# Token mixing and SwiGLU on one core: the taps of the next pair all put among the products, two splits of the first pair put behind three sums, and a new joined order of products and output steps

## The chip, the cores and the metric

The kernel runs on one core of a Trainium2 chip. The metric is the device time of one execution in microseconds (us). The execution shown in the profile took 2447.03 us; three unprofiled runs took 2442.12, 2444.20 and 2449.53 us (median 2444.2).

## What is computed

```python
# lightweight convolution: x is (8, 4096, 192), weight is (8 heads, 7 taps)
w = softmax(weight, axis=-1)
out[b, s, head] = sum over k of w[head, k] * x_pad[b, s + k, head]   # causal, 6 zeros ahead
# then, over the 32768 tokens x of 192 numbers:
xn  = x / sqrt(mean(x * x) + 1e-6) * rms_g
g   = xn @ w_gate            # 192 -> 1536
val = xn @ w_val
return (silu(g) * val) @ w_out   # 1536 -> 192
```

All of it is float32 in and out.

## The kernel before

**Tiling.** The tokens are cut into 32 pairs of 2 x 512 tokens. For a pair, the 1536 hidden columns are six groups j = 0 to 5, each with two blocks of 128 columns. A pair needs 68 products into the hidden columns (six matmuls each, L948) and then 42 output steps (twelve matmul instructions each, L976). Groups 0, 2, 4 and 5 use seven-product forms of Strassen's kind (items P and Q), groups 1 and 3 use the plain form (items A, B, E). The inputs of the products are split into three float32r terms so that sums of the three are exact enough: a high part, a remainder and a second term.

**Joined list.** `LINE` (L131) gives the order of TensorE's 68 products and 42 steps in a pair; a word such as `P7.0` is product P7 of group 0, and `o3.4` is output step form 3 of group 4. TensorE works through this list pair after pair.

**Written order.** `FIRST` (pair 1), `SECOND` (pair 2) and `ORDER` (every later pair) are lists of words that `run` (L1301) emits one after the other. `p3` emits the next three items of the joined list. Every other word goes into the queue of one engine (V VectorE, A ScalarE, G GpSimd, S the sync queue that issues DMAs). A queue is worked in the order in which the words stand, and each instruction waits only for its data and buffers. A trailing `+` means that the word belongs to the next pair, `++` to the one after, `-` to the previous one. So while pair w is multiplied, VectorE also prepares pair w+1, and finishes pair w-1.

The words that matter here:

- `cv0` to `cv6`: the seven taps of the convolution (L470 on ScalarE for `cv0`, L474 on VectorE). Each reads the loaded tokens `xh` and adds into `y`; all wait for the loads `ld.0` to `ld.7` (L174, one per head). Behind the last tap follow `sq`, `red`, `pow`, `bc`, `mul` (the normalisation, in place in `xh`), then `pl.0` to `pl.7` (L1098, eight DMAs that put the heads into DRAM) and `ft.0`, `ft.2`, `ft.4`, `ft.5` (L676, the fetch of the transposed tokens `xb`).
- `x1` to `x4`: sums of token blocks into `tt` (L868). Operands 0, 1 and 2 of the products are token blocks, operands 3 and 4 are these sums.
- `n.i`, `l.i`, `d.i`: the three terms of operand i (ScalarE cast L705, VectorE L854, VectorE L856). A product multiplies with the high part first, then with `l`, then with `d`.
- `f1`, `f3`, `f4`, `f5`, `f6`: copies and sums between banks of products (L705, L1025, L1018); `ga` to `gd` (L1031) and `ma` to `md` (L1038): silu and multiplication of a finished bank, which gives the bank back.
- `h1` to `h4` (L1003): sums of hidden blocks, which the output steps read.
- `c1`, `s7`, `c2` (copies) and `C22`, `C21` (L1055): sums of output banks; `C21` gives back the bank `Z`. `T11`, `T12`, `T21`, `T22` (L991): transposition of finished outputs into `o_sb`; `T12` gives back the bank `X`.
- `st.g.i` (written `Sst0.1-`, L1087): the stores of the previous pair's `o_sb`. In the last pair the stores go out as soon as both transpositions of a half have run (`at_end`, L1069), three on ScalarE's queue and two on the sync queue.
- Split weights sit in DRAM and are loaded into a ring of 12 slots, one piece ahead of its use (`ring_load`, L814): 48 loads in a pair, each behind the last use of its slot.

Two `o_sb` buffers rotate, one for each half of the pair, so a transposition waits for the stores that read the buffer last.

Of the kernel before, what the change touches and what calls it, by code (L numbers as in the profile page):

```python
# [20 lines left out]
def kernel(  # L21
# [58 lines left out]
    )  # L80
    ORDER = (
# [15 lines left out]
    )  # L97
    SECOND = (
# [15 lines left out]
    )  # L114
    FIRST = (
# [14 lines left out]
    )  # L130
    LINE = (  # L131
# [7 lines left out]
    )  # L139

    cst = ctx.enter_context(tc.tile_pool(name="cst", bufs=1))
# [1213 lines left out]
```

## Time and profile before

| | |
|---|---|
| profiled execution, own time | 2447.03 us |
| its span | 2445.2 us |
| around the span | 1.8 us |
| three runs | 2442.12, 2444.20, 2449.53 us |
| TensorE granted clock, whole span | 0.999 |
| busy: TensorE, VectorE, ScalarE, GpSimd | 2427.2, 2089.3, 1034.0, 565.7 us |

A row of a timeline reads: start in us, length in us, engine, line, operation, output and inputs; in brackets how long the engine stood idle before it and who ended the wait. Rows of one kind that follow each other are merged (x2, x3). A row of the chain of waits reads: start, length, what the end of the execution hung on in that time. Names of tiles are shared: `part` is also the space of the three terms of an operand, `ring` also that of pair 2's tokens. Times of successive VectorE rows overlap by some hundredths, so the distance from one start to the next is what an instruction costs the queue.

### The profile page before, as it was taken

The numbers are of one execution on the slowest core, as the hardware profiler recorded it, in microseconds if no ns is written. First come the engines' busy times: TensorE is split into PE (matmuls) and PEld (weight loads), VectorE is DVE, ScalarE is ACT, GpSimd is POOL, SyncE is SP. The second block draws the span as 40 slices with busy tenths as digits, with TensorE's granted clock in tenths as the row PEclk, the third lists the DMA queues.
The fourth block names the chain that finished last, engine by engine and source line by source line (L and its number), as shares of the span: only waits on it lengthen the run. The fifth ranks groups of instructions, "written<-read, shape, count | busy, mean of one in ns | idle before, by whom it ended". The sixth has DMA issues, their size and how long they took to land.

```text
span 2445.2 us, 69382 instructions
## 1 busy us (share of the span) xinstructions
PE 2427.2 (99%) x29136; PEld 1978.5 (81%) x29136; DVE 2089.3 (85%) x2702; ACT 1034.0 (42%) x1431; POOL 565.7 (23%) x482
## 2 busy tenths in 40 slices
PE   8999999999999999999999999999999999999998
PEld 5647888888888888888788898888888788888886
DVE  9678888889888899888898888898888898888974
ACT  6443344444344444344444444443444443444432
POOL 0542122211222211222211222211222112222111
PEclk9999999999999999999999999999999999999999
DMA  7375678777788677778677787777786777876753
GB/s 153 61 212 145 168 177 215 191 170 176 171 186 216 184 170 173 173 196 206 177 173 171 173 210 194 173 175 171 179 215 181 169 173 172 197 204 179 175 155 83
DMA packets 716392, 430.55 MB, mean 176 GB/s; under 512 B 510330, under 2 KB 702386, under 8 KB 716082
## 3 DMA queue, kind: packets, MB, share of 16 engines
q1 hardware_dynamic: 712336, 425.21, 70.7%
q8 instruction: 230, 3.77, 0.7%
q10 hardware_dynamic: 3746, 0.92, 0.2%
q14 instruction: 80, 0.66, 0.1%
HBM read 366.96 MB, written 58.98 MB: 174 GB/s over the span
## 4 chain that ended last, share of the span: by engine, by line
PE 97%; DVE 1%; DMA 1%; SPq 1%; issue 0%; ACT 0%; DVEq 0%; ACTq 0%
PE ps L948 57%; PE ps L976 35%; PE ps L920 2%; PE ps L1135 2%; SPq L174 1%; DMA ht<-in_moe_w_val_dram 0%; DVE part L854 0%; DMA x<-in_x_dram 0%; DVE ht L1003 0%; DMA xh<-in_x_dram 0%; DMA ht<-in_moe_w_gate_dram 0%; SPq L258 0%; DVE part L856 0%; DVE y L474 0%; DVE ht L1038 0%
## 5 line engine op out<-in xcount | busy, mean ns | idle before, releaser
L948 PE MATMUL ps<-part,ring 64*128 64x512 f32 x11160 | 1305.3, 387 | 0.1
L948 PEld LDWEIGHTS ps<-part,ring 64*128 64x128 f32 x11160 | 1108.5, 184 | 161.7 <-issue 5.6
L1031 ACT ACTIVATE tt<-ps 128x512 f32<-128x512 f32 x744 | 441.8, 598 | 683.8 <-PE ps L948 614.8
L1038 DVE TENSOR_TENSOR ht<-ps,tt 128x512 f32<-128x512 f32 x744 | 497.7, 685 | 208.8 <-ACT tt L1031 200.2
L976 PE MATMUL ps<-ht,wo_sb 128*32 128x384 f32 (+2 forms) x7272 | 430.3, 380 | 0.0
L976 PE MATMUL ps<-ht,x 128*32 128x256 f32 (+2 forms) x6696 | 413.1, 379 | 2.8 <-DVE ht L1003 2.6
L976 PEld LDWEIGHTS ps<-ht,wo_sb 128*32 128x32 f32 x7272 | 321.5, 110 | 94.7 <-issue 12.6
L976 PEld LDWEIGHTS ps<-ht,x 128*32 128x32 f32 x6696 | 298.4, 110 | 86.5 <-DVE ht L1003 3.2
L474 DVE SCALAR_TENSOR_TENSOR y<-xh,tp,y 128x1536 f32<-128x1536 f32 x186 | 337.2, 1813 | 3.9 <-ACT y L470 3.5
L503 POOL TENSOR_SCALAR r<-r 128x8 f32<-128x8 f32 x31 | 6.2, 198 | 1431.7 <-DVE r L498 1431.6
L1025 DVE TENSOR_TENSOR ps<-ps,tt 128x1024 f32<-128x1024 f32 x210 | 258.3, 1230 | 36.9 <-ACT tt L705 24.8
L705 ACT COPY ps<-ps 128x1024 f32<-128x1024 f32 (+1 forms) x151 | 134.0, 887 | 274.6 <-PE ps L948 130.1
L1003 POOL TENSOR_TENSOR hs<-ht 128x512 f32<-128x512 f32 x120 | 155.8, 1298 | 169.3 <-DVE ht L1038 127.9
L705 ACT COPY tt<-ps 128x384 f32<-128x384 f32 (+1 forms) x182 | 151.9, 835 | 89.6 <-PE ps L976 79.6
L705 ACT CAST part<-tt 128x1024 fp32r<-128x1024 f32 x60 | 62.8, 1047 | 287.4 <-DVE tt L868 287.4
L1003 DVE TENSOR_TENSOR ht<-ht 128x512 f32<-128x512 f32 x252 | 168.6, 698 | 6.8 <-PE ps L976 6.6
L1003 POOL TENSOR_TENSOR ht<-ht 128x512 f32<-128x512 f32 x120 | 154.4, 1299 | 2.3
L976 PE MATMUL ps<-hs,x 128*32 128x256 f32 (+2 forms) x2232 | 145.2, 379 | 0.0
L948 PE MATMUL ps<-part,part 64*128 64x512 f32 x912 | 128.8, 386 | 0.0
L976 PEld LDWEIGHTS ps<-hs,x 128*32 128x32 f32 x2232 | 106.3, 110 | 24.1
L856 DVE SCALAR_TENSOR_TENSOR part<-part,xb 128x1024 fp32r<-128x1024 f32 x87 | 105.6, 1214 | 0.0
L854 DVE TENSOR_TENSOR part<-xb,part 128x1024 fp32r<-128x1024 f32 x87 | 103.3, 1214 | 0.0
(137 smaller groups left out, 1619.4 us busy)
## 6 DMA issues: line engine op xcount, KB each, us to landing
ring<-wd SPq DMA_DIRECT2D x1326, 192.0 KB
xb<-xd SPq DMA_DIRECT2D x60, 512.0 KB
xd<-xh SPq DMA_DIRECT2D x240, 96.0 KB
part<-wd SPq DMA_DIRECT2D x114, 192.0 KB
xh<-in_x_dram SPq DMA_DIRECT2D x192, 105.0 KB
xb<-xd SPq DMA_DIRECT2D x60, 256.0 KB
out_dram<-o_sb SPq DMA_DIRECT2D x126, 96.0 KB
out_dram<-o_sb SPq DMA_DIRECT2D x62, 128.0 KB
```

Source lines behind the costliest of these rows:

```text
L474: nc.vector.scalar_tensor_tensor(out=y, in0=xk, scalar=w, in1=y, op0=ALU.mult, op1=ALU.add)
L705: nc.scalar.copy(out=dst, in_=src)
L854: e.tensor_tensor(out=split_of(g, 1).bitcast(F32R), in0=src, in1=high, op=ALU.subtract)
L856: nc.vector.scalar_tensor_tensor(out=split_of(g, 2).bitcast(F32R), in0=high, scalar=1.0 + SPLIT, in1=src, op0=ALU.mult, op1=ALU.subtract,)
L920: nc.tensor.matmul(out=self.both(j, c)[:, h, :], lhsT=wf[HALF[h], k, 2 * HOME[j] + f, :], rhs=rb[HALF[h], k, g, :], start=(k == 0), stop=( ...
L948: nc.tensor.matmul(out=self.both(j, c)[:, h, :], lhsT=left[HALF[h]], rhs=right[HALF[h]], start=(first and q == 0), stop=True, skip_group_c ...
L976: nc.tensor.matmul(out=self.acc(b)[i * Q : (i + 1) * Q, at : at + n], lhsT=left, rhs=cols, start=fresh, stop=True, skip_group_check=True, ...
L1003: engine[eng].tensor_tensor(out=dst, in0=a, in1=b, op=op)
L1025: nc.vector.tensor_tensor(out=self.both(j, c), in0=self.both(j, "b"), in1=s5, op=ALU.add)
L1031: nc.scalar.activation(out=tt[:, t, :], in_=self.both(j, c)[:, 0, :], func=AF.Silu)
L1038: nc.vector.tensor_tensor(out=self.hv(j, "abcd".index(c)), in0=self.both(j, c)[:, 1, :], in1=tt[:, t, :], op=ALU.mult,)
L1135: nc.tensor.matmul(out=bank(h, bks[h])[:], lhsT=wf[HALF[h], AT[h][k], u * NF + f, :], rhs=xb[HALF[h], g, k, :], start=(k == 0), stop=(k == ...
```

## The change

`ORDER` is written anew. Two kinds of words change their place by more than a few items. The tap `cv4`, which stood at the end of the list behind `C22` for the pair after next (`Vcv4++`), now stands among the next pair's products (`Vcv4+`); five of the six VectorE taps have another place. The split `l.4` stands at the end of the list and `d.4` at the head of the next, where it was the other way round. `C21` no longer has a tap ahead of it. The transpositions come in the order T22, T21, T12 (before: T12, T21, T22). The token sum `x3` moves ahead of the last multiplications; fetches stand earlier, and the store `st1.2` of the previous pair at the very end, behind all loads of `x`. `SECOND` follows the same pattern. In `FIRST`, `Vd.1+` and `Vl.2+` move behind `Vh1.5`, `Vh3.5` and `Vh2.5`. `LINE` keeps the same items in another order. The number of instructions of each kind does not change.

```diff
     ORDER = (
-        "p3- p1 Vcv5+ Af1.0 p1 VT12- p1 VT21- p1 Vcv1+ VT22- Aga.1 p1 Vma.1 Vl.4 p1 Aga.0 p1",
-        "Af3.0 Vma.0 p4 Vf4.0 p1 Agb.1 Sst0.1- p3 Vcv2+ Vmb.1 p2 Vf5.0 Sst0.2- Agc.0 p1 Vmc.0",
-        "Agd.1 p2 Vmd.1 Agd.0 p2 Agb.0 p1 Vcv6+ Vmb.0 Sst0.3- Vmd.0 p1 Vcv3+ Af1.2 p1 Sst1.0-",
-        "p1 Agc.1 Vmc.1 p1 Sst0.4- Af3.2 Vf4.2 p3 Sst0.0- p1 Aga.2 Sst1.1- p1 Vma.2 Vf5.2 p1",
-        "Asq+ Agc.2 p1 Vred+ p1 Vmc.2 Agd.2 p2 Agb.2 p1 Vmd.2 Gpow+ Agb.3 p1 Vmb.2 p1 Af1.4",
-        "Vmb.3 Vbc+ p2 Gmul+ Aga.3 p1 Spl.4+ p1 Af3.4 Vma.3 p2 Vf4.4 Spl.2+ p1 Spl.7+ Aga.4",
-        "p1 Vma.4 Vh1.1 Spl.5+ p2 Vf5.4 Spl.1+ p1 Agd.3 Vmd.3 Sst1.3- p2 Gh1.0 Agc.4 Spl.3+",
-        "Vmc.4 p1 Spl.0+ Agd.4 p1 Af1.5 Sst1.4- Gh1.3 Agb.4 Gh3.0 Spl.6+ Vmd.4 p1 Gh3.1 Vmb.4",
-        "p2 Sft.0+ Af3.5 Sft.2+ p1 Sft.4+ Gh1.2 p2 Vf4.5 Sld.4++ p2 Sft.5+ Aga.5 Vma.5",
-        "Sld.3++ p1 Agc.3 p1 Vf5.5 Gh3.3 Gh1.4 Vh3.2 p1 Sld.7++ Vmc.3 p2 Vf6.5 Agc.5 p2 Agb.5",
-        "Agd.5 Sld.6++ p1 Vmb.5 p1 Vmd.5 Vmc.5 p1 Vh1.5 Sld.5++ p1 Gh3.4 Vh2.0 Sst1.2- p3 Ac1",
-        "p1 Vh2.3 An.0+ Vh3.5 p2 Vh2.2 Gh2.1 p1 Vx3+ Sld.0++ Vh2.4 p2 Vd.0+ An.1+ p1 Vl.1+",
-        "Vl.0+ p1 Sld.2++ Vx1+ Vh2.5 Vx2+ p2 An.3+ As7 Vh4.2 Vh4.0 Vh4.3 p2 VT11 p1 An.2+ p1",
-        "Vh4.4 Sld.1++ p1 Vh4.1 Vd.2+ p1 Vh4.5 Vl.2+ Vl.3+ Ac2 p2 Vd.1+ p3 Vx4+ p2 An.4+ p1",
-        "Vd.3+ Acv0++ p1 VC22 Vd.4+ Vcv4++ p5 VC21",
+        "Vcv5+ VT22- p1 Af1.0 p2 Vcv3+ p1 VT21- p1 VT12- p1 Vcv1+ Aga.1 p1 Vma.1 Af3.0 Vd.4",
+        "Vf4.0 p3 Vcv4+ p1 Aga.0 p1 Vma.0 p5 Agb.1 Sst0.3- Vmb.1 Sst0.1- Agc.0 Vf5.0 Vmc.0 p2",
+        "Agd.1 Vcv2+ p2 Agb.0 Sst1.3- Sst0.2- Agd.0 Vmd.1 Vmb.0 Vh1.1 p1 Vmd.0 p1 Af1.2 p1",
+        "Vcv6+ p1 Agc.1 Vmc.1 p4 Af3.2 Vf4.2 Aga.2 p1 Vma.2 Vf5.2 p1 Sst1.1- Asq+ p3 Vred+ p2",
+        "Agd.2 Agc.2 Vmd.2 Gpow+ p1 Agb.2 Vmc.2 p2 Vmb.2 Agb.3 p1 Af1.4 Sst0.4- Vmb.3 p1 Vbc+",
+        "p1 Aga.3 p1 Gmul+ p1 Spl.0+ Af3.4 p1 Spl.4+ Spl.3+ Vma.3 Aga.4 p1 Vf4.4 p1 Gh1.2",
+        "Sst1.4- Vma.4 p2 Spl.2+ Spl.1+ Vh3.2 p1 Agd.3 Spl.5+ p1 Agc.4 Spl.6+ Vf5.4 Vmd.3 p1",
+        "Spl.7+ Vmc.4 p2 Agd.4 Sft.0+ Sft.2+ p1 Gh1.3 Sld.5++ Af1.5 Vmd.4 p2 Agb.4 Af3.5 p1",
+        "Sld.7++ Vmb.4 Sft.4+ Sst0.0- p1 Sft.5+ p1 Sld.4++ Vf4.5 p1 Aga.5 Gh3.1 p1 Agc.3 p2",
+        "Vma.5 p1 Gh1.0 Sst1.0- Vf5.5 p1 Sld.3++ Vmc.3 Vf6.5 p2 Vx3+ Gh1.4 p2 Agb.5 Agd.5",
+        "Vmb.5 Agc.5 p2 Vmd.5 p1 Gh3.3 Gh3.0 Vmc.5 Vh1.5 p3 Sld.1++ An.0+ p1 Ac1 Vh3.5 Vx1+",
+        "p1 Vh2.3 Vd.0+ p1 Gh3.4 p3 Vh2.2 Vh2.0 An.1+ p1 Vx2+ Gh2.1 An.3+ Vh2.5 p2 Sld.6++ p1",
+        "Vd.1+ p1 Vh4.5 p2 As7 Sld.0++ An.2+ Vh2.4 Vh4.0 Sld.2++ p1 Vl.1+ p1 Vh4.2 Vl.0+",
+        "Vh4.3 VT11 p2 Vh4.4 Vd.2+ p1 Vl.3+ Ac2 Vh4.1 p2 Vl.2+ p3 Vx4+ p1 Vd.3+ p3 An.4+ VC22",
+        "p1 Acv0++ p3 Vl.4+ p2 VC21 p1 Sst1.2-",
     )
     SECOND = (
...
     FIRST = (
...
-        "An.2+ p1 Vd.3+ p1 Agb.5 Vd.2+ Vmb.5 Sld.0++ p1 Vl.3+ p2 Vl.1+ Agc.5 Vmc.5 Vd.1+ p1",
-        "Sld.1++ Vl.2+ p6 Sld.2++ Agd.5 p1 Vmd.5 Gh2.0 Gh2.4 Gh2.2 Gh2.3 Gh2.1 p1 Vh1.5 p2",
-        "Ac1 Sld.3++ Vh3.5 Vh2.5 Sld.4++ Sld.5++ Sld.6++ Sld.7++ Acv0++ An.0+ An.4+ Gl.0+",
+        "An.2+ p1 Vd.3+ p1 Agb.5 Vd.2+ Vmb.5 Sld.0++ p1 Vl.3+ p2 Vl.1+ Agc.5 Vmc.5 p1 Sld.1++",
+        "p6 Sld.2++ Agd.5 p1 Vmd.5 Gh2.0 Gh2.4 Gh2.2 Gh2.3 Gh2.1 p1 Vh1.5 p2 Ac1 Sld.3++",
+        "Vh3.5 Vh2.5 Vd.1+ Vl.2+ Sld.4++ Sld.5++ Sld.6++ Sld.7++ Acv0++ An.0+ An.4+ Gl.0+",
         "Vd.0+ p4 Vh4.5 p1 Vh4.0 R p3 As7 p6 Ac2 Vh4.3 Vcv1++ Vcv2++ p8 Vh4.2 p2 Vh4.1 p2",
         "VC21 p1 Vh4.4",
     )
     LINE = (
-        "P1.0 Aa.1 Ea.1 Ba.1 P2.0 Q1.0 P5.0 P6.0 Ab.1 Eb.1 Bb.1 Ad.1 P3.0 P7.0 Q2.0 Ed.1 Bd.1",
+        "P1.0 Aa.1 Ea.1 Ba.1 P2.0 P5.0 P6.0 Q1.0 Ab.1 Bb.1 Eb.1 P7.0 Q2.0 P3.0 Ad.1 Bd.1 Ed.1",
...
-        "o2.4 o7.0 o6.2 o6.4 o6.1 o6.5 o4.1 o6.0 o4.0 o4.4 o5.4 o5.5 o5.0 o5.2 o4.5 o5.1 o5.3",
-        "o4.3 o4.2 o3.4 o3.3 o3.1 o3.0 o3.2 o3.5",
+        "o6.1 o6.0 o6.5 o2.3 o6.3 o2.1 o6.4 o4.2 o4.4 o5.1 o5.4 o5.0 o5.3 o4.3 o5.5 o5.2 o4.5",
+        "o4.1 o4.0 o3.2 o3.4 o3.1 o3.0 o3.5 o3.3",
     )
```

38 rows, old and new, of tables (LINE, SECOND) are left out of this document.

## Prediction

> **What bounds the kernel now.** I read the page's first part, then the chain of waits in order of time, TensorE's waits, and then timelines where the chain leaves TensorE.
>
> ```profile
> span 2445.2 us, 69382 instructions
> PE 2427.2 (99%) x29136; PEld 1978.5 (81%) x29136; DVE 2089.3 (85%) x2702; ACT 1034.0 (42%) x1431; POOL 565.7 (23%) x482
> ```
>
> TensorE is busy 99% of the span and the change removes none of its instructions, so only its 18 us of idle time, delays that count as busy, and the ends of the run can change. The chain shows pair after pair as 46.5 us of products and 27.4 us of output steps:
>
> ```profile
> 288.36 46.50 PE ps L948 x408
> ...
> 953.90 46.51 PE ps L948 x408
> ...
> 1101.99 46.50 PE ps L948 x408
> ...
> 1167.45 4.32 DMA xh<-in_x_dram
> ...
> 1175.50 0.48 DVE tt L1055
> ...
> 1176.02 47.15 PE ps L948 x408
> ...
> 1918.84 47.15 PE ps L948 x408
> ...
> 2363.68 46.53 PE ps L948 x408
> ```
>
> An undisturbed pair takes (953.90 - 288.36) / 9 = 73.95 us. The 28 pairs from 288.36 to 2363.68 take 2075.32 us, and 28 x 73.95 = 2070.6: scattered delays cost only 4.7 us in this execution. Two product stages, at 1176.02 and 1918.84, are 0.64 us longer each: 1.3 us. The first shows its cause: the token load lands at 1167.45 + 4.32 = 1171.77, 69.8 us after that pair began; tap 0 on ScalarE follows, then a tap on VectorE, and only behind it `C21` (L1055), which gives the next products their bank. I cannot put the other 3.4 us down to one cause.
>
> **First pair: `d.1` and `l.2` go behind three sums.** TensorE's waits and both timelines around 190 us:
>
> ```profile
> PE ps L976 <- DVE ht L1003: 2.6, 2, 1.4
> 184.48 9.71 POOL L1003 TENSOR_TENSOR ht<-hs,ht 128x512 f32<-128x512 f32 x5 [7.53 <-PE ps L976]
> 187.43 1.71 DVE L856 SCALAR_TENSOR_TENSOR part<-part,ring 128x1024 fp32r<-128x1024 f32 x1
> 192.00 1.07 DVE L1003 TENSOR_TENSOR hs<-ht 128x512 f32<-128x512 f32 x1
> 193.10 1.64 DVE L1003 TENSOR_TENSOR ht<-ht 128x512 f32<-128x512 f32 x1
> 194.80 1.51 PE L976 MATMUL ps<-ht,x 128*32 128x384 f32 x24 [1.35 <-DVE ht L1003]
> 194.85 2.67 DVE L1003 TENSOR_TENSOR ht<-hs,ht 128x512 f32<-128x512 f32 x1
> 197.57 4.76 PE L976 MATMUL ps<-ht,x 128*32 128x384 f32 x84 [1.26 <-DVE ht L1003]
> L1003 DVE TENSOR_TENSOR ht<-ht 128x512 f32<-128x512 f32 x252 | 168.6, 698 | 6.8 <-PE ps L976 6.6
> ```
>
> TensorE wants `h3.5` at 194.80 - 1.35 = 193.45, and `h2.5` two steps (2 x 27.4 / 42 = 1.3) later, at 194.76. Afterwards `md.5` starts at 187.43, where `d.1` did, the sums start at about 188.05 (L1038 takes 0.64, below), and with the durations above (1.07, 1.64, 2.67) `h3.5` is ready at about 190.8 and `h2.5` at 193.5. Both waits go: -2.6 us. The two splits then run until about 197.5, the time at which the sums ended before (194.85 + 2.67), since the queue holds the same work; TensorE needs them in pair 2's second group of products, after 213. The bound: if each sum takes the dearest duration (2.67), `h2.5` is ready at 188.05 + 3 x 2.67 = 196.06, 1.3 us late, and 1.3 are won. I take 2.6, since the sums run beside the same GpSimd work (busy until 194.2) as in the rows.
>
> [...]
>
> **The end of the run.** With the order T22, T21, T12 the half that is complete early is stored early.
>
> ```profile
> 2437.70 0.65 DVE L991 STREAM_TRANSPOSE o_sb<-ps 128x256 f32<-128x256 f32 x2 [3.34 <-PE ps L976]
> 2438.18 4.29 ACTq L1087 DMA_DIRECT2D out_dram<-o_sb  x6
> ```
>
> Before, VectorE stood 3.34 us idle, from 2434.4, because `T12`, which waits for TensorE's last step, stood first; then ten stores went out together, six on ScalarE's queue (4.29 us, 0.72 each), and 2445.2 - 2442.47 = 2.7 us later the span ended. Afterwards T22 and T21 run in the idle time (at most 0.65 us each), three of the six are issued from about 2435.5 to 2437.7, and three remain behind `T12`: 3 x 0.72 = -2.1 us. The bounds are 0 (should the landing of the last store set the end) and -2.7 (should the stores also land sooner).
>
> **The steady part.** The stages of an undisturbed pair and its queues (in steps of 73.95 from 288.36 it began at 510.2, the next at 584.15):
>
> ```profile
> 556.70:584.10 27.40, 27.40 (x507) 20.91 (x506) 26.89 (x36) 8.87 (x11) 1.30 (x1) 1.00 0.73 140
> 555.68 1.22 DVE L1018 TENSOR_TENSOR ps<-ps,tt 128x1024 f32<-128x1024 f32 x1
> 579.54 1.21 DVE L856 SCALAR_TENSOR_TENSOR part<-part,tt 128x1024 fp32r<-128x1024 f32 x1
> 580.68 1.80 DVE L474 SCALAR_TENSOR_TENSOR y<-xh,tp,y 128x1536 f32<-128x1536 f32 x1
> 582.41 0.54 DVE L1055 TENSOR_TENSOR tt<-ps,tt 128x384 f32<-128x384 f32 x1
> 584.60 0.63 DVE L991 STREAM_TRANSPOSE o_sb<-ps 128x256 f32<-128x256 f32 x2
> 587.93 0.64 DVE L1038 TENSOR_TENSOR ht<-ps,tt 128x512 f32<-128x512 f32 x1
> 590.24 1.22 DVE L1025 TENSOR_TENSOR ps<-ps,tt 128x1024 f32<-128x1024 f32 x1
> 579.01 1.58 ACT L470 ACTIVATE y<-xh,tp 128x1536 f32<-128x1536 f32 x1
> 541.01 0.58 SPq L1098 DMA_DIRECT2D xd<-xh  x1
> 552.37 3.45 SPq L676 DMA_DIRECT2D xb<-xd  x2
> 561.19 2.00 ACT L705 CAST part<-xb 128x1024 fp32r<-128x1024 f32 x2
> ```
>
> In the output stage VectorE is busy 26.89 of 27.4 us; a tap there costs 582.41 - 580.68 = 1.73. Taking `cv4` out lets `C21` end 1.73 us sooner than at 582.95, at 581.2; its last input comes a few steps earlier in the new list, so it may be 0.3 sooner still, 580.9. `d.4` against `l.4` is an exchange of 1.2 for 1.2. In an undisturbed pair `C21` was in time anyway, so this wins nothing.
>
> What the tap costs among the products: VectorE's queue from `C21` on is now cv5, T22, cv3, T21, T12, cv1, `ma.1`, `d.4`, `f4.0`, cv4, `ma.0`. From 580.9: four taps 4 x 1.73, three transpositions 3 x 0.63, `ma.1` 0.64, `d.4` 1.14 (580.68 - 579.54), `f4.0` 1.22, `ma.0` 0.64, in all 12.45, ending at 593.35. The product that needs the bank of `ma.0`, `Ad.1`, is the 15th of the new list: 584.15 + 14 x 46.51 / 68 = 593.7. The margin is 0.35 us, somewhat more since rows that follow each other overlap. `f4.0` ends at 592.7 less the tap `cv4`, 591.0, and `P7.0`, the 12th, comes at 591.7. So nothing waits, but these margins are thin. Behind `ma.0` the list repeats the old distances.
>
> The token sum `x3` now stands behind `f6.5` (555.68 + 1.2 = 556.9) and ahead of the last multiplications, where it stood 5 us later. It needs fetch 0. Before, 19 DMAs from 541.01 to the fetch at 552.37 took 0.60 each; the new list has 14 there (eight puts, five ring loads, a store), so the fetch goes out at about 549.4. The cast that reads it ran at 561.19, at most 8.8 us after its issue, which bounds the landing at 558.2, 1.3 us late; the other bound is 0.5 MB at the 140 GB/s of this stage, 3.7 us, or 553.1. I take the latter, since the cast stood behind another copy and not behind the DMA.
>
> The store `st1.2` goes behind the loads of `x`, where only T22 of the next window waits for it, and two 96 KB stores move into the stretch of the loads from ahead of it; one ring load (192 KB) leaves that stretch. So the tokens land no later, and tap 0 may end some 0.65 us later than at 580.59 (0.3 until `cv5`, and the 0.35 above). Before, tokens that landed at 69.8 us, 1.0 after the usual start of tap 0 (579.01 - 510.2 = 68.8), cost 0.64. I take 1.0 of the 1.3 us of late loads as won, bounds 0 and 1.3, and leave the other 3.4 as they are, bounds 0 and -3.4.
>
> **The sum.** -2.6 - 2.1 - 1.0 = -5.7 on the execution's own 2447.0 (2445.2 and 1.8 around it): 2441.3. Without its 4.7 us of scatter that execution would be at 2442.3, and the fastest run took 2442.12; the median run, 2444.2, therefore holds about 2 us of scatter, of which the same share, 1.0 / 4.7, is 0.4. Against the median: 2444.2 - 2.6 - 2.1 - 0.4 = **2439.1**.
>
> **Rivals.** (1) *VectorE too late among the products (slower).* Its place is the 0.35 us before `Ad.1`. If tap 0 ends more than 0.65 us later than now in ordinary pairs, or `x3` holds up the queue as by the bound, every further microsecond recurs in 29 pairs, since VectorE has no idle time from `x3` to `ma.0`. At `x3`'s bound, 1.3 - 0.35 = 0.95 us: 2439 + 28 = 2467. For it speaks how dense the queue is; against it that the fetch goes out 3 us sooner.
> (2) *Only the end is won.* The sums take their dearest durations (1.3 of 2.6) and late loads stay as they are: 2444.2 - 1.3 - 1.2 = 2441.7, and 2444 if the landing of the last store sets the end. The steady order, for all its moves, is then worth nothing, as the gapless chain suggests. [...]
> (3) *The scatter goes as well.* If earlier fetches and the later store thin out the DMA traffic so that no delay is left, the median comes down to the floor: 2442.2 - 4.7 = 2437.5, and with the outer bound of the end 2436.9 or less. For it speaks that the scatter sits in stages crowded with DMAs; against it that the bytes stay the same.
>
> **How the numbers follow.** Forecast 60%, (1) 13%, (2) 13%, (3) 14%. A measurement of this kernel can tell about 0.3%, 7.3 us: faster means below 2436.9, slower above 2451.5. Rival (1) is slower, (3) and the lower edge of the forecast give 17% of faster, and the rest, 70%, is within 0.3%. The range reaches from 2435.5 (both outer bounds) to 2447 (case 2 with some of (1)).
>
> **What would show it.** In the profile after: no wait of TensorE for L1003 near 195 us; the store issues on ScalarE's queue in two groups, the first before TensorE ends; `C21` about 2 us before each pair; product stages of 46.5 us at all pair starts. Wrong would be a product stage or a wait for L1038 that lengthens every pair beyond 73.95 us, or a VectorE wait for the fetch ahead of `x3`.

## The result, and the profile after

Eleven executions of the changed kernel took 2438.37 us in the median (2437.19 to 2441.18), eleven of the kernel before on the same chip 2445.12 us (2442.12 to 2449.53). The ratio is 0.9972, with a 95% interval from 0.9964 to 0.9980. The predicted 2439.1 us is 0.7 us off, and the range holds the time. How the terms of the sum came out is another matter.

The page of the changed kernel, its span and its busy times:

```profile
span 2437.5 us, 69194 instructions
PE 2423.9 (99%) x29136; PEld 1905.5 (78%) x29136; DVE 2099.9 (86%) x2702; ACT 1026.5 (42%) x1431; POOL 564.4 (23%) x482
```

The span fell by 2445.2 - 2437.5 = 7.7 us, with the same 29136 matmuls. Three places make it up. The chain of waits after (start, length, what the end hung on):

```profile
183.60 23.54 PE ps L976 x288
207.13 1.58 PE ps L948 x12
...
285.30 46.52 PE ps L948 x408
...
507.15 39.19 PE ps L948 x343
546.35 5.82 DMA part<-wd
552.17 0.04 issue
552.21 3.01 PE ps L948 x24
...
1914.17 46.91 PE ps L948 x408
...
2358.18 46.46 PE ps L948 x408
```

*First pair.* Pair 3 begins at 285.30, before at 288.36: -3.06, of which 2.99 are won by the end of the first output stage (207.13, before 210.12). The timeline around its waits:

```profile
184.32 1.22 DVE L854 TENSOR_TENSOR part<-ring,part 128x1024 fp32r<-128x1024 f32 x1
...
184.52 8.52 POOL L1003 TENSOR_TENSOR ht<-hs,ht 128x512 f32<-128x512 f32 x5 [7.54 <-PE ps L976]
...
186.77 1.72 DVE L1003 TENSOR_TENSOR hs<-ht 128x512 f32<-128x512 f32 x1
...
188.52 1.66 DVE L1003 TENSOR_TENSOR ht<-ht 128x512 f32<-128x512 f32 x1
...
190.29 1.60 DVE L1003 TENSOR_TENSOR ht<-hs,ht 128x512 f32<-128x512 f32 x1
...
193.22 6.00 PE L976 MATMUL ps<-ht,x 128*32 128x384 f32 x106
```

The three sums are done at 191.9 and TensorE runs through 193.22 without a bracket. Before, its two waits stood there as 1.35 and 1.26. They cost more than these brackets: by the distances from start to start it was 1.59 and 1.46, 3.05 us in all, because the end that the trace gives a matmul here lies some 0.2 us behind the start of the next (1.59 - 1.35, 1.46 - 1.26).

*Steady part.* From 285.30 to 2358.18 the 28 pairs take 2072.9 us (before 2075.3): -2.4. Every output stage is 27.44 us long, while some of before were longer by 0.1 to 1.0. What is left of the scatter sits among the products: once 1.5 us behind a ring piece that landed late (546.35 + 5.82 = 552.17, product P3.5), and 0.4 us in the pair at 1914.17.

*End.* From the start of `T12` the span lasts 2437.5 - 2432.12 = 5.4 us instead of 7.5: -2.1. The timeline:

```profile
2428.70 1.15 DVE L991 STREAM_TRANSPOSE o_sb<-tt 128x256 f32<-128x256 f32 x4
...
2429.69 5.10 ACTq L1087 DMA_DIRECT2D out_dram<-o_sb  x6
...
2432.12 0.65 DVE L991 STREAM_TRANSPOSE o_sb<-ps 128x256 f32<-128x256 f32 x2 [2.28 <-PE ps L976]
```

T22 and T21 run at 2428.70, and ScalarE's queue begins its six stores 2.4 us ahead of `T12`, where before it began 0.5 us behind it.

-3.1 - 2.4 - 2.1 is -7.6 of the 7.7. All three have the sign that was predicted. But a profile is one execution, so the runs below ask what each part is worth as a rule.

### The profile page after: what moved, and what is told of

The parts are those of the page before. It is cut to its first block, busy times and chain, and to the rows that moved or that the text cites. A ratio compares the mean times of both kernels' runs of the same rounds, so it can differ in the third digit from the quotient of the medians.

```text
span 2437.5 us, 69194 instructions
## 1 busy us (share of the span) xinstructions
PE 2423.9 (99%) x29136; PEld 1905.5 (78%) x29136; DVE 2099.9 (86%) x2702; ACT 1026.5 (42%) x1431; POOL 564.4 (23%) x482
## 3 DMA queue, kind: packets, MB, share of 16 engines
q8 instruction: 230, 3.77, 0.7%
## 4 chain that ended last, share of the span: by engine, by line
PE 98%; DMA 1%; SPq 0%; DVE 0%; issue 0%; DVEq 0%
PE ps L948 57%; PE ps L976 36%; PE ps L920 3%; PE ps L1135 2%; DMA ht<-in_moe_w_val_dram 0%; SPq L174 0%; DMA part<-wd 0%; DMA x<-in_x_dram 0%; DMA ht<-in_moe_w_gate_dram 0%; SPq L258 0%; DVE y L441 0%; DVE part L324 0%; DVE part L329 0%; DVE part L332 0%; DVE part L364 0%
## 5 line engine op out<-in xcount | busy, mean ns | idle before, releaser
L948 PEld LDWEIGHTS ps<-part,ring 64*128 64x128 f32 x11214 | 1059.6, 184 | 215.5 <-issue 6.0
L1031 ACT ACTIVATE tt<-ps 128x512 f32<-128x512 f32 x744 | 434.2, 597 | 714.9 <-PE ps L948 649.4
L976 PE MATMUL ps<-ht,wo_sb 128*32 128x384 f32 (+2 forms) x7272 | 437.7, 380 | 0.0
L1025 DVE TENSOR_TENSOR ps<-ps,tt 128x1024 f32<-128x1024 f32 x210 | 258.7, 1232 | 52.6 <-PE ps L948 23.6
L1003 POOL TENSOR_TENSOR hs<-ht 128x512 f32<-128x512 f32 x120 | 155.2, 1294 | 176.9 <-DVE ht L1038 176.9
L1003 DVE TENSOR_TENSOR ht<-ht 128x512 f32<-128x512 f32 x252 | 176.7, 703 | 6.8 <-PE ps L976 5.6
L1003 POOL TENSOR_TENSOR ht<-ht 128x512 f32<-128x512 f32 x120 | 152.7, 1293 | 0.0
L976 PE MATMUL ps<-hs,x 128*32 128x128 f32 (+2 forms) x2232 | 141.8, 379 | 0.0
L976 PEld LDWEIGHTS ps<-hs,x 128*32 128x32 f32 x2232 | 100.6, 110 | 28.4
L948 PE MATMUL ps<-part,part 64*128 64x512 f32 x816 | 116.4, 386 | 0.0
```

Of the source, the lines that this page charges most:

```text
L948: nc.tensor.matmul(out=self.both(j, c)[:, h, :], lhsT=left[HALF[h]], rhs=right[HALF[h]], start=(first and q == 0), stop=True, skip_group_c ...
L976: nc.tensor.matmul(out=self.acc(b)[i * Q : (i + 1) * Q, at : at + n], lhsT=left, rhs=cols, start=fresh, stop=True, skip_group_check=True, ...
L1003: engine[eng].tensor_tensor(out=dst, in0=a, in1=b, op=op)
L1025: nc.vector.tensor_tensor(out=self.both(j, c), in0=self.both(j, "b"), in1=s5, op=ALU.add)
L1031: nc.scalar.activation(out=tt[:, t, :], in_=self.both(j, c)[:, 0, :], func=AF.Silu)
```

## The experiments

Each run names the kernel it starts from. Times and ratios are against the kernel before in the same group of runs. "28 pairs" is the time from the first product of pair 3 to that of pair 31 in the run's profile. "First pair" is the time from the first output step of pair 1 to the first product of pair 3. In three of the runs the file is one line shorter, in one five lines longer, and their line numbers are shifted by as much.

### The three parts, alone and left out

The kernel before with the changed `FIRST` alone:

```diff
-        "An.2+ p1 Vd.3+ p1 Agb.5 Vd.2+ Vmb.5 Sld.0++ p1 Vl.3+ p2 Vl.1+ Agc.5 Vmc.5 Vd.1+ p1",
-        "Sld.1++ Vl.2+ p6 Sld.2++ Agd.5 p1 Vmd.5 Gh2.0 Gh2.4 Gh2.2 Gh2.3 Gh2.1 p1 Vh1.5 p2",
-        "Ac1 Sld.3++ Vh3.5 Vh2.5 Sld.4++ Sld.5++ Sld.6++ Sld.7++ Acv0++ An.0+ An.4+ Gl.0+",
+        "An.2+ p1 Vd.3+ p1 Agb.5 Vd.2+ Vmb.5 Sld.0++ p1 Vl.3+ p2 Vl.1+ Agc.5 Vmc.5 p1 Sld.1++",
+        "p6 Sld.2++ Agd.5 p1 Vmd.5 Gh2.0 Gh2.4 Gh2.2 Gh2.3 Gh2.1 p1 Vh1.5 p2 Ac1 Sld.3++",
+        "Vh3.5 Vh2.5 Vd.1+ Vl.2+ Sld.4++ Sld.5++ Sld.6++ Sld.7++ Acv0++ An.0+ An.4+ Gl.0+",
```

> The kernel before with the new FIRST only (d.1 and l.2 behind the three sums). Theory: the first pair's share of the gain is its own: TensorE's two waits for L1003 vanish, pair 3's products start 2.6 to 3.0 us sooner than 288.36, and the median falls by the same. [...] The steady pairs and the end stay as before.

Measured: 2446.34 us against 2447.28, ratio 1.0000 (0.9991 to 1.0009). The waits for L1003 are gone from its profile, but the time is the same within 2.2 us. The interval leaves out the 2.6 of the prediction; it does not leave out its lower bound of 1.3.

The kernel before with the transpositions of the last window alone in the new order, and the changed kernel with them in the old order:

```diff
+    END = {"VT12-": "VT22-", "VT22-": "VT12-"}
     for w in range(3, PAIRS + 1):
-        run([w for row in ORDER for w in row.split()], w)
+        words_w = [x for row in ORDER for x in row.split()]
+        run([END.get(x, x) if w == PAIRS else x for x in words_w], w)
```

> The kernel before with T22 and T12 exchanged in the last window only (T22, T21, T12). Theory: the time from TensorE's last step to the end of the span falls from 7.5 us to about 5.4, so 2.1 us are won, and nothing else moves. Rival: the landing of the last store sets the end and 0 are won.

> The changed kernel with T12, T21, T22 again in the last window only. Theory: the end after TensorE's last step is 7.5 us again, 2.1 us slower than the changed kernel. Rival: 0, if the end was shortened by something else.

Measured: alone 2444.99, ratio 0.9992 (0.9983 to 1.0001), or -2.0; the changed kernel without it 2440.37, ratio 0.9977 (0.9967 to 0.9987). The interval is as wide as the term, and the profiles are sharper: the time from the start of `T12` in the last window to the end of the span is 7.4 to 7.5 us in all eight profiles with the old order there, and 5.3 to 5.4 in all six with the new one. The -2.1 is a fixed gain.

The changed kernel with the old `FIRST`:

> The changed kernel with the FIRST of before. Theory: 2.6 to 3.0 us slower than the changed kernel (about 2441.2 where that is 2438.4), with TensorE's two waits for L1003 back. Rival: the steady order gives them back later and the difference is under 1 us.

Measured: 2439.82 us, ratio 0.9971 (0.9960 to 0.9983). Without its share of the first pair the kernel still wins 7.1 us. The two waits did not come back as expected: its profile has one of 0.3 us there, and beside the 6.8 and 8.3 us that the changed kernel itself won in two other groups the loss comes to 1.2 us or less, where 2.6 to 3.0 were expected; each of these figures is uncertain by some 2 us or more.

Then the steady order without the other two, and the changed kernel itself in the same group of runs:

```diff
     FIRST = (
...
-        "Vh3.5 Vh2.5 Vd.1+ Vl.2+ Sld.4++ Sld.5++ Sld.6++ Sld.7++ Acv0++ An.0+ An.4+ Gl.0+",
+        "Ac1 Sld.3++ Vh3.5 Vh2.5 Sld.4++ Sld.5++ Sld.6++ Sld.7++ Acv0++ An.0+ An.4+ Gl.0+",
...
+    END = {"VT12-": "VT22-", "VT22-": "VT12-"}
     for w in range(3, PAIRS + 1):
-        run([w for row in ORDER for w in row.split()], w)
+        words_w = [x for row in ORDER for x in row.split()]
+        run([END.get(x, x) if w == PAIRS else x for x in words_w], w)
```

> The steady order alone: the first pair and the last window's transpositions as before. By the prediction the steady order is worth 0.4 (1.0 in the profiled execution), so 2446.7 where the kernel before takes 2447.1, and 28 pairs in 2074.3 us. By the rival (the scatter goes) it is worth 3.4 to 4: 2443.4, and 28 pairs in 2071 to 2073 us. The first pair of before stands in it: TensorE waits for L1003 near 195 us 2.6 us if that wait belongs to the order, 0.3 us if it comes only when a GpSimd sum begins just ahead of a split on VectorE, as the first four runs suggest.

> The changed kernel itself, beside the versions that change one part, for one common yardstick. Expected as before: 5 to 8 us below the kernel before, 28 steady pairs in 2071 to 2073 us, first pair without a wait for L1003.

Measured, with the kernel before at 2447.30: the steady order alone 2441.46, ratio 0.9978 (0.9969 to 0.9987), or -5.4 us; the changed kernel 2438.83, ratio 0.9966 (0.9953 to 0.9978), or -8.3. The steady order, which the prediction put at -0.4, is the largest of the three.

### Why the first pair is worth less than its profile showed

Eight profiles have the old `FIRST`. Two more of them, that of the end alone and that of a run described below (the puts of the changed kernel in the kernel before):

```profile
184.89 1.22 DVE L854 TENSOR_TENSOR part<-ring,part 128x1024 fp32r<-128x1024 f32 x1
...
185.12 9.97 POOL L1003 TENSOR_TENSOR ht<-hs,ht 128x512 f32<-128x512 f32 x5 [7.53 <-PE ps L976]
...
194.06 1.58 DVE L1003 TENSOR_TENSOR ht<-hs,ht 128x512 f32<-128x512 f32 x1
```

```profile
185.12 9.74 POOL L1002 TENSOR_TENSOR ht<-hs,ht 128x512 f32<-128x512 f32 x5 [7.53 <-PE ps L975]
...
185.25 2.31 DVE L853 TENSOR_TENSOR part<-ring,part 128x1024 fp32r<-128x1024 f32 x1
...
195.51 2.67 DVE L1002 TENSOR_TENSOR ht<-hs,ht 128x512 f32<-128x512 f32 x1
```

In the first the split starts 0.23 us ahead of GpSimd's first sum and takes 1.22. In the second it starts 0.13 us behind and takes 2.31, everything behind it on VectorE is later, and TensorE waits 2.6 us for the sums instead of 0.3. The profiled execution of the kernel before was of the second kind (its split at 184.60 took 2.30, GpSimd began at 184.48). In six of the eight profiles the split comes first, by 0.04 to 0.32 us, and the first pair takes 102.3 to 102.6 us; in two GpSimd comes first, and it takes 104.8 and 105.5 (of the latter 0.7 is a delay elsewhere, in pair 2's output stage). With the new `FIRST` five profiles read 101.7 to 101.8, also one in which GpSimd came first; a sixth, with more work put into every pair (`d.4` twice, below), reads 102.6. So the new order wins about 3.1 us in some executions and 0.7 in most; over these eight it is (6 x 0.7 + 2 x 3.1) / 8 = 1.3 in the mean. Eight profiles are few, so the share of the dear executions, and with it the 1.3, is rough.

In these rows the engine that comes second takes longer, by somewhat less than the other still has to run. In the second profile GpSimd's first sum, the first of the five merged ones, took 1.36 us by itself, so 1.23 of it were left when the split came, and the split took 2.31 - 1.22 = 1.09 more. In the profile of before GpSimd's first sum took 1.34, 1.22 of it were left, and the split took 2.30 - 1.22 = 1.08 more. The other way round, where the split comes first, GpSimd's first sum takes 2.04 to 2.33 us.

### What in the steady order takes the scatter away

First the tap ahead of `C21` and the order of the DMAs, each alone in the kernel before:

```diff
-        "Vd.3+ Acv0++ p1 VC22 Vd.4+ Vcv4++ p5 VC21",
+        "Vd.3+ Acv0++ p1 VC22 Vd.4+ p5 VC21 Vcv4++",
```

> The kernel before with one word moved: the tap cv4 of the output stage goes behind C21. If the tap ahead of C21 is what makes the scatter (C21 gives the next products their bank, and a late tap makes it late), the delays at the start of the product stages go and 28 pairs take 2073 us or less, 2.5 to 3.5 less than the 2075.3 to 2076.6 of the versions with the old order: about 2444. If the order of the DMAs is what counts, the late tokens still cost 1 us or more and 28 pairs stay at 2075 us or more.

All words of the sync queue (puts, fetches, loads and stores) at the items of the joined list where the changed `ORDER` has them; the word lists of this queue alone, from the first put on:

```diff
-Spl.4+ Spl.2+ Spl.7+ Spl.5+ Spl.1+ Sst1.3- Spl.3+ Spl.0+ Sst1.4- Spl.6+ Sft.0+ Sft.2+ Sft.4+ Sld.4++
+Spl.0+ Spl.4+ Spl.3+ Sst1.4- Spl.2+ Spl.1+ Spl.5+ Spl.6+ Spl.7+ Sft.0+ Sft.2+ Sld.5++ Sld.7++ Sft.4+
...
```

> The kernel before with only the DMA words of SyncE's queue at the places of the changed list. If the order of the DMAs makes the scatter, 28 pairs fall from 2075.3 to 2076.6 us to 2072 or 2073 and the time to about 2444; if the tap ahead of C21 makes it, they stay at 2075 us or more. The late ring piece at P3.5 should then show here as it does in the changed kernel (up to 1.5 us in a pair), since the eight puts stand together.

Measured: `C21` first 2444.21 against 2447.30, ratio 0.9991 (0.9982 to 1.0000), 28 pairs in 2080.5 us in its profiled execution, the slowest of its eleven (2450.27), and delays between output steps as before (eight of them). Its products also waited three times for a multiplication, 2.6 us in all, as the tap now stands behind `C21` and ahead of their multiplications. The DMA order 2441.10, ratio 0.9975 (0.9965 to 0.9984), 28 pairs in 2072.1, and no such delay. So the order of the DMAs alone does what the whole steady order does (0.9978). One expectation failed: P3.5 did not wait here. In the old list P3.5 stands one product (0.68 us) later, which may be why.

This profile still has late tokens:

```profile
1460.80 4.79 DMA xh<-in_x_dram
...
1469.79 47.15 PE ps L948 x408
```

Then the DMA words in two parts, in the kernel before. Only the puts and fetches at their new places (behind @ the number of items of the joined list ahead of a word):

```diff
-Spl.4+@43 Spl.2+@46 Spl.7+@47 Spl.5+@48 Spl.1+@50 Spl.3+@53 Spl.0+@54 Spl.6+@55 Sft.0+@58 Sft.2+@58 Sft.4+@59 Sft.5+@63
+Spl.0+@44 Spl.4+@45 Spl.3+@45 Spl.2+@49 Spl.1+@49 Spl.5+@50 Spl.6+@51 Spl.7+@52 Sft.0+@54 Sft.2+@54 Sft.4+@58 Sft.5+@59
```

> The kernel before with only the puts and fetches of the tokens (eight 96 KB puts, four fetches) at the places of the changed list, about 4 us earlier; loads and stores stay. If their place thins out the DMAs at 48 to 56 us of a pair, where the instruction fetches of TensorE start late, the delays between output steps go and 28 pairs take 2072 to 2073 us, the time about 2441. If not, 28 pairs stay at 2075 us or more, and the late token loads (0.5 us each in two to four pairs) stay in either case.

Only the loads and stores at their new places; those that move by eight items or more:

```diff
-Sst1.0-@25 Sst0.4-@27 Sst0.0-@30 Sst1.3-@51 Sst1.4-@55 Sld.7++@66 Sld.6++@70 Sld.5++@73 Sst1.2-@74 Sld.0++@81 Sld.1++@91
+Sst1.3-@21 Sst0.4-@40 Sst1.4-@47 Sld.5++@55 Sld.7++@58 Sst0.0-@58 Sst1.0-@65 Sld.1++@76 Sld.6++@85 Sld.0++@89 Sst1.2-@107
```

> The kernel before with only the input loads and output stores at the places of the changed list (one 96 KB store behind the last load, two others later); puts and fetches stay. If these make the scatter, 28 pairs take 2072 to 2073 us here and 2075 or more with the puts and fetches alone. Theory: both parts give some of it, the loads and stores the part of the late tokens (1 to 1.5 us), the puts and fetches the delays between output steps (2 to 3 us).

Measured: puts and fetches alone 2442.28 against 2446.56, ratio 0.9984 (0.9975 to 0.9993). Its 28 pairs take 2071.0 us, with one late token and no delay between output steps; its profiled execution also has the dear first pair (the second fence above). Loads and stores alone 2456.01, ratio 1.0040 (1.0026 to 1.0054): slower. TensorE's waits and the timeline there:

```profile
PE ps L976 <- DVE tt L1055: 8.3, 11, 1.0
```

```profile
796.53 1.05 ACT L705 CAST part<-xb 128x1024 fp32r<-128x1024 f32 x1 [3.09 <-DMA xb<-xd]
...
797.62 1.23 DVE L856 SCALAR_TENSOR_TENSOR part<-part,xb 128x1024 fp32r<-128x1024 f32 x1 [2.10 <-ACT part L705]
...
805.11 3.24 PE L976 MATMUL ps<-ht,wo_sb 128*32 128x384 f32 x54 [1.04 <-DVE tt L1055]
```

The loads now go out ahead of the fetches, the fetched tokens come 3.09 us after the cast could have started, VectorE stands 2.10 us behind the cast, and the sum of banks that TensorE needs is late by 1.0. So the new places of loads and stores cost time unless the fetches go out earlier too. The expectation that both parts give some of the gain was wrong: the loads and stores alone lose time, and the puts and fetches alone bring the 28 pairs down as far as the whole DMA order does (2071.0 and 2072.1 us). Their ratio, 0.9984, is less than the 0.9975 of the whole DMA order, but the two intervals overlap.

What the vanished delays were shows in rows where TensorE stops with no data to wait for, here in the kernel before. The second row is a queue of instructions, in packets of 3.77 MB / 230 = 16.4 KB. TensorE has 29,136 matmuls, as many weight loads and 709 waits and drains in this trace, 58,981 rows, which makes 58,981 / 230 = 256 to a packet; by that count it is taken here for TensorE's queue:

```profile
1750.93 2.74 PEld L976 LDWEIGHTS ps<-ht,wo_sb 128*32 128x32 f32 x52 [0.72 <-issue]
```

```profile
q8 instruction: 230, 3.77, 0.7%
```

Four profiles with the old DMA order (before, first pair alone, end alone, `C21` first) have 20 delays of 0.15 us or more between output steps of pairs 3 to 30. The table sets some of them beside the end of the last instruction packet ahead, in us; the last column is the distance from the same packet to the same place of the list in five profiles with the whole changed DMA order:

```
execution         pair  step        lost   packet ended before   in the five others
before             22   15th o2.3   0.66          1.9            4.4 5.1 3.9 5.3 3.5
C21 first          22   15th o2.3   0.66          2.6            the same place
end alone          22   25th o6.0   0.80          1.4            3.9 4.7 4.1 4.3 4.2
before             24   21st o6.4   0.80          1.9            1.4 2.7 4.2 2.7 2.2
before             30   18th o2.4   0.28          2.2            2.4 3.8 3.3 3.1 2.2
C21 first          30   18th o2.4   0.32          2.0            the same place
first pair alone    4   24th o4.1   1.22          1.5            3.7 5.3 6.0 4.7 4.1
C21 first          18   24th o4.1   0.48          2.0            3.7 4.7 4.7 3.7 4.0
```

All 20 resume 1.3 to 2.6 us after an instruction packet has ended, where only 18% of all output steps begin at that distance from one, and different executions stop at the same step of the same pair, though every pair runs the same list. The traces hold a sharper sign. If TensorE's rows are counted from the start of the program (weight loads, matmuls and semaphore waits), the weight load at which it goes on has, in all 20 delays, 193 or 194 rows of a block of 256 ahead of it; a delay of another kind would hit these two places one time in 128. So TensorE stops each time at the same place of its instruction packets, and it goes on soon after one has landed: by these signs the delays are waits for the next 256 instructions.

In the kernel before, the packets 48 to 56 us into a pair begin late: by the same count of rows, less 256 for each packet ahead, TensorE is at row 288 when such a packet begins (median of 30), and at 196 for the 172 others of the 28 pairs. In the changed kernel it is at 232 (28 packets) and 194 (174). What makes such a packet late is not shown. The nine profiles with the whole DMA order changed or with the puts and fetches moved have no such delay, so the place of these DMAs is enough to take them away. But the loads and stores alone have none either: in that run's output stages the weight loads stop 18 times, and each time elsewhere in the block. And the DMA engines are nearly as busy without the delays as with them: 48 to 56 us into a pair their share is 1.08 to 1.09 in four profiles without, 1.11 to 1.12 in the four with. No run changed the packets alone.

The delays between steps are not the whole gain of the steady part. In three profiles with the old order (before, first pair alone, end alone) and the five above with the new one, the 28 pairs differ by 4.0 us: 1.7 are these delays, 1.1 the last steps ahead of a new pair, and 1.2 lie among the products. Tap 0 ended 0.3 us or more later than usual in 4, 6 and 7 of 27 pairs with the old order, in none to two with the new one, and in one with the puts and fetches alone.

An output step has 24 instructions and takes 27.44 / 42 = 0.65 us, so 256 of them last 6.9 us there. The 20 delays lost 0.17 to 1.22 us each.

### The margin, and a version with less of the last wait

The changed kernel with `d.4` issued twice, to the same place with the same values:

```diff
                 op0=ALU.mult, op1=ALU.subtract,
             )
+            if g == 4:
+                nc.vector.scalar_tensor_tensor(
+                    out=split_of(g, 2).bitcast(F32R)[:, 0:2], in0=high[:, 0:2],
+                    scalar=1.0 + SPLIT, in1=src[:, 0:2], op0=ALU.mult, op1=ALU.subtract,
+                )
```

> The changed kernel with the split d.4 issued twice in each pair: 1.14 us more on VectorE ahead of the bank that the 15th product needs. By the prediction's margin of 0.35 us every pair loses 0.79 us, in 28 to 29 pairs 22 to 23 us: 2461. By the distance read from the trace after (bank ready at about 591.6, product at 592.3, some 0.55 us) 0.6 a pair: 2455. If VectorE's queue is slack there, nothing.

Measured in two executions: 2467.03 against 2446.56, ratio 1.0085 (1.0067 to 1.0104), more than either figure expected. Its 28 pairs take 2097.5 us, 25.7 more than the 2071.8 of the changed kernel in the group above, or 0.92 a pair. TensorE's waits and the place in one pair (L861 is the added split, and L1030 here is L1025, which writes the bank that P7.0 needs):

```profile
PE ps L953 <- DVE ps L1030: 7.6, 30, 0.3
```

```profile
892.44 1.23 DVE L861 SCALAR_TENSOR_TENSOR part<-part,tt 128x1024 fp32r<-128x1024 f32 x1
893.59 1.23 DVE L1030 TENSOR_TENSOR ps<-ps,tt 128x1024 f32<-128x1024 f32 x1
...
894.87 4.65 PE L953 MATMUL ps<-part,ring 64*128 64x512 f32 x36 [0.31 <-DVE ps L1030]
```

Start to start, TensorE loses 0.54 us at P7.0 and the product behind it in the median pair, another 0.27 at `Ad.1` and the one behind it, and 0.08 later on. The margins themselves stand in the traces of the changed kernel: in the median pair `f4.0` ends 0.90 us ahead of P7.0 and `ma.0` 0.62 us ahead of `Ad.1`. The prediction had 0.7 and 0.35. It had the right two places and that they are thin, and made them 0.2 to 0.3 us too thin.

The changed kernel with two puts behind four ring loads:

```diff
-        "Sst1.4- Vma.4 p2 Spl.2+ Spl.1+ Vh3.2 p1 Agd.3 Spl.5+ p1 Agc.4 Spl.6+ Vf5.4 Vmd.3 p1",
-        "Spl.7+ Vmc.4 p2 Agd.4 Sft.0+ Sft.2+ p1 Gh1.3 Sld.5++ Af1.5 Vmd.4 p2 Agb.4 Af3.5 p1",
+        "Sst1.4- Vma.4 p2 Spl.2+ Spl.1+ Vh3.2 p1 Agd.3 Spl.5+ p1 Agc.4 Vf5.4 Vmd.3 p1 Vmc.4",
+        "p2 Agd.4 Spl.6+ Spl.7+ Sft.0+ Sft.2+ p1 Gh1.3 Sld.5++ Af1.5 Vmd.4 p2 Agb.4 Af3.5 p1",
```

> The changed kernel with two of the eight puts behind four ring loads instead of ahead of them. The ring piece that P3.5 needs then goes out 1.1 us sooner (two issues of 0.55), so the waits at P3.5 (0.3 to 1.5 us in an execution of the changed order) go: 28 pairs in 2070 to 2071.5 us and 2438 where the changed kernel takes 2438.8. If fetch 0, now behind these loads as well, is late for x3, a wait shows ahead of x3 and pairs get longer.

Measured: 2436.97 (2436.37 to 2437.93) against 2446.56, ratio 0.9963 (0.9950 to 0.9975). The waits at P3.5 are gone from its profile, and 28 pairs take 2070.0 us. It is the lowest time of the study; its interval overlaps that of the changed kernel, so that it beats that one rests on its profile. One disturbed pair is left:

```profile
1172.10 47.26 PE ps L947 x408
```

There tap 0 ended 1.96 us before the pair began, where 3.84 is usual, so `f4.0` and `ma.0` were 1.1 us late. The same pair was late in this way in two more profiles with the new order (the changed kernel beside the experiments, and the one with the old end), for 0.5 to 1.0 us.

## Why the prediction was right, and where it was not

**First pair, -2.6.** In the profiled execution the mechanism came as written: the sums first, the waits gone, the splits in time. There it won 3.0, since each wait cost some 0.2 us more than its bracket. The step that failed is the scaling: the 2.6 was carried from one profile to the median of the runs. That wait stood in two of eight profiles; in the mean of the eight the term is about 1.3, and 0.7 in most. The prediction took the profiled execution without its scatter as a floor and concluded that "the median run, 2444.2, therefore holds about 2 us of scatter". That floor held this wait of about 2.4 us too, which most executions do not have, so the conclusion does not follow. The number 1.3 is also that of rival (2), but not for its reason: the three sums took 1.6 to 1.7 us each, not their dearest 2.67.

**End, -2.1.** Right, in size and mechanism, and the same in every profile.

**Steady part, -0.4 in the median.** Right in most of what was worked out. Rows of VectorE and of the sync queue in the changed kernel:

```profile
578.84 0.55 DVE L1055 TENSOR_TENSOR tt<-ps,tt 128x384 f32<-128x384 f32 x1
```

```profile
547.48 1.33 SPq L676 DMA_DIRECT2D xb<-xd  x2
```

`C21` ends at 579.4, 3.3 us ahead of the products at 582.66 (predicted 2.9 to 3.3, before 1.2), and by itself that won nothing clear of noise (0.9991, 0.9982 to 1.0000). The fetch for `x3` goes out 40.3 us into the pair at 507.15 (predicted 39.2, before 42.2), and nothing waits ahead of `x3`. The margins held, save in single pairs. The step that failed is "and leave the other 3.4 as they are". The steady part won 2.4 us in this pair of profiles and 4.0 in the mean: 28 pairs took 2075.3, 2075.6 and 2076.6 us in three profiles with the old order, and 2072.9, 2071.8, 2072.3, 2071.3 and 2070.9 in five with the new one. Of the 4.0, 1.7 were delays between output steps, and they were not random: all fell 54 to 63 us into a pair at the same place of a block of 256 instructions, and they went when DMAs moved. The argument against rival 3, that the bytes stay the same, was true and beside the point, since moving them in time was enough.

**The sum.** By the runs it is -1.3 - 2.1 - 4.0 = -7.4, against the -5.1 of the prediction and the measured -6.8 (0.9972) and -8.3 (0.9966). That the predicted time was only 0.7 us off is in part luck: one term was 1.3 too large and another 3.6 too small, and the base was low as well, 2444.2 from three runs where eleven give 2445.1.

**The rivals.** (1), VectorE too late among the products, came only in single pairs with late tokens, but 1.14 us more work there brought it in every pair: 0.92 us each. (2) is excluded by the steady order alone (0.9978). Its sum in the prediction does not come out: it takes 1.2 for the end, which the same text puts at 2.1; with that it would be 2444.2 - 1.3 - 2.1 = 2440.8. (3), the scatter goes as well, is what happened, nearly in full; it named DMA traffic as the cause, and the runs bear that out, though not that there is less of it.

## What to carry to other kernels

Here the delays of the bounding engine that had no data wait went with its instructions: all 20 ended 1.3 to 2.6 us behind a packet of the instruction queue, at row 193 or 194 of 256. For such a delay look whether both hold, and then try other places for the transfers around it. Before a wait of one profile enters a forecast for the median, ask whether it hangs on which of two engines starts first by 0.1 us; the one here stood in two of eight profiles. A rewrite of many queues is best split by queue: here the sync queue's words alone gave the gain of the steady part (0.9975 against 0.9978), and the loads and stores among them alone made the kernel slower (1.0040).

## What the runs showed of the hardware that was not expected

A VectorE split that started 0.12 and 0.13 us behind a GpSimd sum took 2.30 and 2.31 us, and 1.22 when it started 0.04 us or more ahead of it; by that, one engine's start moved the whole first pair by some 2.4 us (104.8 against 102.3 to 102.6). TensorE stopped 20 times for 0.17 to 1.22 us between steps whose data were ready, at the same places of the program in different executions, and each time 193 or 194 rows into a block of 256. The stage of 28 matmuls at 5 us (L558) took 4.61 us in the profile of before and 5.20 us in that of the changed kernel, whose code is the same there, so that even the first microseconds differed by 0.6 us between these two executions.
